# Dynamic convolution and squared-ReLU FFN on one core: band matmuls for the convolution, and a 64-row split of the first FFN matmul

## The chip, the cores and the metric

One core of a Trainium2 chip runs the whole program. The metric is device time in microseconds from start to end; lower is better. The engines named below work side by side, each through its own instructions in its own order, and wait for each other by semaphores: TensorE (PE, matmuls; PEld, its weight loads), VectorE (DVE), ScalarE (ACT), GpSimd (POOL) and SyncE (SP, which only issues DMA transfers here).

## What is computed

A causal convolution of 7 taps whose weights are different at each token and head, then an FFN with a squared ReLU. B = 8 sequences of S = 4096 tokens, D = 192 features in 8 heads of 24, FFN width 2048.

```
w = exp(weight_gen - max); w = w / sum(w)              # [B, S, 8 heads, 7 taps]
x_pad = 6 zero rows in front of x                      # [B, S + 6, 192]
y[b, s, h, g] = sum over k of w[b, s, h, k] * x_pad[b, s + k, 24 h + g]
h = maximum(y.reshape(32768, 192) @ w_in, 0)           # w_in  [192, 2048]
out = (h * h) @ w_out                                  # w_out [2048, 192]
```

## The kernel before

The 32768 tokens are cut into 64 blocks of 512 (8 per sequence); a block is four chunks of 128 tokens. One loop runs over blocks as a software pipeline: in one turn block `it` is loaded and its weights are normalised, block `it - 1` is convolved, block `it - 2` transposed, block `it - 3` goes through the first FFN matmul and block `it - 4` through the second.

The convolution has tokens on partitions. A transfer brings `x` seven times, shifted by one token each (`X6`, 128 x 7 x 192 per chunk, L112; at the start of a sequence seven transfers, L101). GpSimd normalises the weights (L129) and multiplies all seven copies by them (`pk`, L140, 1344 products per partition). VectorE adds the seven in three steps in place (L152 576, L155 384, L158 192 elements). TensorE transposes the sum, eight 128x128 pieces a block (L169), so that features lie on partitions, and ScalarE copies it out of PSUM (`yt`, L179). There are two `pk` buffers, and the transposes are their last readers, so a product waits for the transposes of two blocks before.

The FFN has features on partitions. The first matmul (mm1, L188) makes 16 chunks of 128 hidden units for 512 tokens; the 192 features are taken as 128 and as 64 that are padded with 64 zero rows of `w_in` to 128, so each chunk is two full matmuls, 32 a block. A pair of chunks is one `hps` tile of two PSUM banks (three buffers). ScalarE applies the ReLU to a pair (`t1`, L204, four buffers), VectorE squares it (`gT`, L209). The second matmul (mm2, L219) has a 128x128 piece of `gT` as weights and `w_out` as moving operand with 192 columns, 64 a block; ScalarE copies the result out (`o_sb`, L230) and SP stores it (L237).

The program is written stage by stage; a scheduling layer then orders the instructions of each engine and sets the waits. All transfers but the FFN weights go through SP's queue.

## Time and profile before

| | us |
|---|---|
| time, median of 2 runs (1389.41 and 1390.3) | 1389.86 |
| span of the profiled execution | 1387.2 |
| TensorE matmuls busy | 937.2 (68%) |
| VectorE busy | 1070.5 (77%) |
| ScalarE busy | 632.5 (46%) |
| GpSimd busy | 725.6 (52%) |
| moved by DMA | 211.26 MB, mean 152 GB/s |
| mean granted TensorE clock | 0.836 of full speed |

The span is that of one execution recorded by the profiler; the time is measured without it. Busy time counts an instruction from its start to its end, also where it is held up inside. A matmul's recorded length includes the time that its result takes to come out, so matmuls in a row overlap, and what a row of them costs is the step from one start to the next.

### The profile page before, as it was taken

How to read it: one execution, taken by the hardware profiler on the slowest of the kernel's cores; microseconds unless marked ns; L12 is line 12 of the kernel's file. 1: busy time of each engine (PE TensorE's matmuls, PEld its weight loads, DVE VectorE, ACT ScalarE, POOL GpSimd, SP SyncE). 2: the span in 40 equal slices, each digit the busy share in tenths (PEclk: the TensorE clock that was granted, in tenths of full speed). 3: DMA queues.
4: the chain of work that ended last, by engine and by line, in shares of the span. 5: the costliest groups of instructions: out<-in, count | busy, mean ns of one | idle time of the engine just before them, and what ended most of it. 6: DMA issues, size and time to landing. Idle time of an engine off the chain costs nothing.

```text
span 1387.2 us, 17548 instructions
## 1 busy us (share of the span) xinstructions
PE 937.2 (68%) x6656; PEld 627.6 (45%) x6656; DVE 1070.5 (77%) x1417; ACT 632.5 (46%) x769; POOL 725.6 (52%) x329
## 2 busy tenths in 40 slices
PE   0376666766766766767767668668667667677688
PEld 0144443544544544534535435435445445444456
DVE  2989778778787787787787787787887877877863
ACT  0244444544544544444444445445445445444455
POOL 3766545646546546456456455455465465464430
PEclk9888888878888888788788878888888888788899
DMA  8524456554443543444443443544434434434001
GB/s 240 218 101 153 144 194 242 192 176 143 159 179 120 173 177 128 166 143 144 181 161 129 166 167 139 183 149 140 177 137 158 176 119 177 173 107 179 15 24 41
DMA packets 114053, 211.26 MB, mean 152 GB/s; under 512 B 42264, under 2 KB 82032, under 8 KB 113968
## 3 DMA queue, kind: packets, MB, share of 16 engines
q1 hardware_dynamic: 111680, 208.57, 42.2%
q0 software_dynamic: 2288, 1.57, 0.8%
q8 instruction: 52, 0.85, 0.3%
q14 instruction: 33, 0.27, 0.1%
HBM read 186.52 MB, written 25.17 MB: 153 GB/s over the span
## 4 chain that ended last, share of the span: by engine, by line
DVE 52%; PE 25%; POOL 12%; ACT 6%; issue 3%; SPq 1%; DMA 1%; POOLq 0%; ACTq 0%; DVEq 0%
DVE pk L152 17%; DVE pk L155 16%; PE o L219 16%; DVE pk L158 13%; POOL pk L140 12%; PE hps L188 9%; DVE gT L209 5%; ACT t L204 4%; ACT o_sb L230 2%; SPq L112 1%; DMA wg<-in_weight_gen_dram 1%; SPq L101 1%; DVE ssum L121 0%; PE yps L169 0%; DVE rcp L124 0%
## 5 line engine op out<-in xcount | busy, mean ns | idle before, releaser
L140 POOL TENSOR_TENSOR pk<-X,nrm 128x1344 f16<-128x1344 f32 x256 | 672.1, 2655 | 511.5 <-ACT o_sb L230 469.0
L188 PE MATMUL hps<-yt,w_in 128*128 128x512 f16 x2048 | 526.3, 408 | 374.1 <-ACT t L204 373.0
L204 ACT ACTIVATE t<-hps 128x1024 f16<-128x1024 f32 x512 | 489.8, 1028 | 424.7 <-DVE gT L209 403.0
L188 PEld LDWEIGHTS <-w_in 128*128 128x128 f16 x2048 | 206.3, 101 | 620.7 <-issue 425.7
L152 DVE TENSOR_TENSOR pk<-pk 128x576 f16<-128x576 f16 x256 | 264.1, 1032 | 231.6 <-POOL pk L140 231.6
L219 PE MATMUL o<-w_out,gT 128*128 128x192 f16 x4096 | 421.3, 268 | 8.5 <-DVE gT L209 7.3
L219 PEld LDWEIGHTS <-gT 128*128 128x128 f16 x4096 | 395.3, 108 | 65.4 <-issue 45.4
L209 DVE TENSOR_TENSOR gT<-t 128x1024 f16<-128x1024 f16 x512 | 344.4, 711 | 28.3 <-ACT t L204 24.8
L155 DVE TENSOR_TENSOR pk<-pk 128x384 f16<-128x384 f16 x256 | 249.4, 974 | 6.3
L158 DVE TENSOR_TENSOR pk<-pk 128x192 f16<-128x192 f16 x256 | 207.5, 811 | 6.2
L230 ACT COPY o_sb<-o 128x384 f32<-128x384 f32 x128 | 61.2, 478 | 266.4 <-PE o L219 266.4
L129 POOL TENSOR_TENSOR nrm<-e,rcp 128x224 f32<-128x224 f32 x64 | 50.5, 789 | 91.8 <-DVE rcp L124 65.7
L169 PE MATMUL yps<-ident,pk 128*128 128x128 f16 x512 | 42.2, 222 | 63.9 <-DVE pk L158 63.9
L179 ACT COPY yt<-yps 128x1024 f16<-128x1024 f16 x64 | 64.8, 1012 | 31.6 <-PE yps L169 31.6
L169 PEld LDWEIGHTS <-pk 128*128 128x128 f16 x512 | 33.5, 98 | 69.8 <-POOL pk L140 59.0
L121 DVE TENSOR_REDUCE ssum<-e 128x32 f32<-128x224 f32 x64 | 24.2, 377 | 26.0 <-ACT e L117 26.0
L117 ACT ACTIVATE e<-wg 128x224 f32<-128x224 f32 x64 | 24.5, 383 | 28.3 <-DMA wg<-in_weight_gen_dram 28.3
L124 DVE RECIPROCAL rcp<-ssum 128x32 f32<-128x32 f32 x64 | 22.5, 352 | 5.3 <-DVE ssum L121 0.5
L98 DVE MEMSET X<- 6x1152 f32 x8 | 8.1, 1018 | 1.4 <-issue 1.2
L58 DVE MEMSET w_in<- 64x1024 uint32 x1 | 0.9, 912 | 1.0 <-PEq L298 1.0
L117 ACT ACT_TABLE_LOAD x1 | 1.3, 1283 | 0.7 <-PEq L298 0.7
L63 POOL DMA_DIRECT2D w_out<-in_moe_w_out_dram x1 | 1.2, 1208 | 0.0
(8 smaller groups left out, 2.2 us busy)
## 6 DMA issues: line engine op xcount, KB each, us to landing
X<-in_x_dram SPq DMA_DIRECT2D x248, 672.0 KB
out_dram<-o_sb SPq DMA_DIRECT2D x128, 192.0 KB
wg<-in_weight_gen_dram SPq DMA_DIRECT2D x64, 112.0 KB
X<-in_x_dram SPq DMA_DIRECT2D x8, 96.0 KB
w_out<-in_moe_w_out_dram POOLq DMA_DIRECT2D x1, 768.0 KB, 18.3
X<-in_x_dram SPq DMA_DIRECT2D x8, 95.2 KB
X<-in_x_dram SPq DMA_DIRECT2D x8, 94.5 KB
X<-in_x_dram SPq DMA_DIRECT2D x8, 93.8 KB
```

What stands on the lines that cost most here:

```text
L129: nc.gpsimd.tensor_tensor(out=nrm, in0=e_t[j], in1=rcp_t[j].unsqueeze(-1).broadcast_to((P, NCH, H, KK)), op=AluOp.mult,)
L140: nc.gpsimd.tensor_tensor(out=pk[:, c], in0=x6_t[j][:, c].rearrange("p k (h g) -> p k h g", h=H), in1=nrm_t[j][:, c] .rearrange("p h k -> ...
L152: nc.vector.tensor_tensor(out=v[:, 0:3, :], in0=v[:, 0:3, :], in1=v[:, 4:7, :], op=AluOp.add)
L155: nc.vector.tensor_tensor(out=v[:, 0:2, :], in0=v[:, 0:2, :], in1=v[:, 2:4, :], op=AluOp.add)
L158: nc.vector.tensor_tensor(out=v[:, 0], in0=v[:, 0], in1=v[:, 1], op=AluOp.add)
L169: nc.tensor.transpose(out=yps[:, ci, c * P : (c + 1) * P], in_=y16[:, dd0 : dd0 + P], identity=ident,)
L179: nc.scalar.copy(out=yt16, in_=yps)
L188: nc.tensor.matmul(out=hps[:, jj, :], lhsT=w_in16[ci][:, fc * P : (fc + 1) * P], rhs=yt16[:, ci, :], start=(ci == 0), stop=(ci == len(d_ch ...
L204: nc.scalar.activation(out=t1, in_=hps_t[(j, fp)], func=ActF.Relu)
L209: nc.vector.tensor_tensor(out=gT[:, 2 * fp : 2 * fp + 2, :], in0=t1, in1=t1, op=AluOp.mult)
L219: nc.tensor.matmul(out=o2[:, c % 2, :], lhsT=gT[:, fc, c * P : (c + 1) * P], rhs=w_out16[:, fc, :], start=(fc == 0), stop=(fc == NF - 1),)
L230: nc.scalar.copy(out=o_sb, in_=o2_t[(j, half)])
```

## The change

The convolution becomes a matmul. For a tile of tokens a band matrix `bd` is built per head: row = input token, column = output token, entry = the softmax weight of that pair where the two are 0 to 6 apart, else 0. With `x` of that tile as weights (tokens on partitions) the matmul gives y transposed at once, features on partitions. A block of 512 tokens is five tiles whose 128 input rows begin 98 tokens apart and which give 104, 104, 96, 96 and 112 outputs. A head has 24 features and TensorE's output places are 32 partitions wide, so each place takes two matmuls: all 32 rows with the later head's band, then the first 24, 16 or 8 rows again with the earlier head's, which overwrite. The last 64 features are made twice, on partitions 0 to 63 and 64 to 127. That is 5 x 16 = 80 matmuls a block, in four 32-column places.

The weights for the band are normalised for a whole sequence at once, written to `vbuf` in a skewed layout of 8 slots (slot = token modulo 8, so that a row's seven weights lie where its column has them), stored to a scratch tensor in DRAM (`vd`, SP) and read back per tile (`wr`, SP). VectorE multiplies them by a constant 0/1 `mask`, both operands repeated by access pattern, five products a block. `x` comes as 16-bit numbers through GpSimd's DMA queue, which converts. ScalarE's copy of y becomes a VectorE cast out of PSUM.

In mm1 the zero padding goes: the 64 rows of `w_in` stand twice in `w_b`, and the upper 64 features of the two chunks of a pair are two matmuls in the array's upper and lower 64 rows. The order is written anew as well: mm1 of a pair of chunks alternates with 8 matmuls of mm2 of the block before, and the convolution of the next block stands behind the sixth pair. PSUM: `h` two buffers of two banks (three before), `o` two (one before), `yp` one of two banks.

The lines that are only removed are those printed above. Of the new ones:

```diff
+    NT = 5
+    STEP = 98
+    BASE = -8
+    starts = [BASE + STEP * i for i in range(NT)]
+    bounds = [0, 104, 208, 304, 400, TB]
...
+    def load_weights():
+        nc.gpsimd.dma_start(out=w_a, in_=moe_w_in[0:P, :])
+        nc.gpsimd.dma_start(out=w_b[0:LO, :], in_=moe_w_in[P:D, :])
+        if ROW_TILED:
+            nc.gpsimd.dma_start(out=w_b[LO:P, :], in_=moe_w_in[P:D, :])
+        else:
+            nc.vector.memset(w_b[LO:P, :], 0.0)
+        nc.gpsimd.dma_start(out=w_o, in_=moe_w_out.rearrange("(c p) m -> p c m", p=P))
...
+    def st_softmax(b):
+        wg = wg_t[b]
+        v = vbuf[b % 2]
+        nc.scalar.activation(out=wg, in_=wg, func=ActF.Exp)
+        ssum = p_sm.tile([P, RH, H], f32, name="ssum")
+        nc.vector.tensor_reduce(out=ssum, in_=wg, axis=AxisX, op=AluOp.add)
+        rcp = p_sm.tile([P, RH, H], f32, name="rcp")
+        nc.vector.reciprocal(out=rcp, in_=ssum)
...
+            nc.vector.tensor_tensor(
+                out=vo,
+                in0=wg[:, i0 : i0 + n],
+                in1=rcp[:, i0 : i0 + n].unsqueeze(-1).broadcast_to((P, n, H, KK)),
+                op=AluOp.mult,
+            )
...
+    def st_load(j):
+        b, t0 = j // NBB, (j % NBB) * TB
+        xt = p_x.tile([P, NT, D], f16, name="xt")
+        wr = p_wr.tile([P, NT, H, SL], f16, name="wr")
+        x_t[j], wr_t[j] = xt, wr
+        wr2 = wr.rearrange("p t h c -> p t (h c)")
+        vd = vd_t[b]
...
+            else:
+                eng.dma_start(out=dst, in_=rows(src, t0 + BASE, width))
+
+    def st_band(j, i):
+        if i == 0:
+            bd_t[j] = p_bd.tile([P, H * TB], f16, name="bd")
+        lo, hi = bounds[i], bounds[i + 1]
+        n = hi - lo
+        m = mask[:, lo:hi]
+        if i == 0 and j % NBB == 0:
+            m = mask0
+        nc.vector.tensor_tensor(
+            out=bd_t[j][:, H * lo : H * hi].rearrange("p (h m c) -> p h m c", h=H, c=SL),
+            in0=wr_t[j][:, i].unsqueeze(2).broadcast_to((P, H, n // SL, SL)),
+            in1=m.rearrange("p (m c) -> p m c", c=SL)
+            .unsqueeze(1)
+            .broadcast_to((P, H, n // SL, SL)),
+            op=AluOp.mult,
+        )
+
+    G = D // H
+    quads = []
+    for q in range(D // 32):
+        ha, hb = (32 * q) // G, (32 * q + 31) // G
+        quads.append((q, ha, hb, hb * G - 32 * q))
+
+    def st_conv(j):
+        yp = ps_y.tile([P, 2, TB], f32, name="yp")
+        yp_t[j] = yp
+        places = [(q, 0, 32 * q) for q in range(4)]
+        places += [(q, 1, 32 * (q - 4)) for q in (4, 5)]
+        places += [(q, 1, 32 * (q - 2)) for q in (4, 5)]
+        for i in range(NT):
+            lo, hi = bounds[i], bounds[i + 1]
+            bd = bd_t[j][:, H * lo : H * hi].rearrange("p (h c) -> p h c", h=H)
+            for later in (True, False):
+                for q, ci, p0 in places:
+                    _, ha, hb, pre = quads[q]
+                    m = 32 if later else pre
+                    nc.tensor.matmul(
+                        out=yp[p0 : p0 + m, ci, lo:hi],
+                        lhsT=x_t[j][:, i, 32 * q : 32 * q + m],
+                        rhs=bd[:, hb if later else ha, :],
+                        start=True,
+                        stop=True,
+                        skip_group_check=True,
+                        tile_position=(0, p0),
...
+    def st_y_evac(j):
+        y = p_y.tile([P, 2, TB], f16, name="y")
+        y_t[j] = y
+        nc.vector.tensor_copy(out=y, in_=yp_t[j])
...
+            nc.tensor.matmul(
+                out=h[:, jj, :], lhsT=w_a[:, fc * P : (fc + 1) * P], rhs=y[:, 0, :],
+                start=True, stop=False,
+            )
...
+        if ROW_TILED:
+            for jj in range(2):
+                fc = 2 * fp + jj
+                r0 = LO * jj
+                nc.tensor.matmul(
+                    out=h[:, jj, :],
+                    lhsT=w_b[r0 : r0 + LO, fc * P : (fc + 1) * P],
+                    rhs=y[r0 : r0 + LO, 1, :],
+                    start=False, stop=True,
+                    tile_position=(r0, 0),
+                )
...
+    def st_mm2(j, part):
+        c, half = part // 2, part % 2
+        if part % 4 == 0:
+            o_t[(j, c // 2)] = ps_o.tile([P, 2, Dm], f32, name="o")
+        o = o_t[(j, c // 2)]
+        for fc in range(half * NF // 2, (half + 1) * NF // 2):
+                out=o[:, c % 2, :],
+                lhsT=g_t[j][:, fc, c * P : (c + 1) * P],
+                rhs=w_o[:, fc, :],
+                start=(fc == 0), stop=(fc == NF - 1),
+            )
...
+        for j in range(NBLK + 1):
+            nb = j // NBB + 1
+            if j < NBLK and nb < B:
+                if j % NBB == 0:
+                    st_wg_load(nb)
+                if j % NBB == 2:
+                    st_softmax(nb)
+            if j + 3 < NBLK:
+                st_load(j + 3)
+            for fp in range(NFP):
+                if j < NBLK:
+                    st_mm1(j, fp)
+                    st_relu(j, fp)
+                if j >= 1:
+                    st_mm2(j - 1, fp)
+                if j < NBLK:
+                    if j + 1 < NBLK:
+                        if fp < NT:
+                            st_band(j + 1, fp)
+                        if fp == NT:
+                            st_conv(j + 1)
+                            st_y_evac(j + 1)
+                    st_sq(j, fp)
```

TensorE, in the middle of a block. Before (`w_in_1` are the padded rows), where mm1 runs in one stretch:

```order
L219 MATMUL o_878<-w_out_68,gT 128x192
L188 LDWEIGHTS w_in_1_65
L188 MATMUL hps<-yt_690,w_in_1_65 128x512
L188 LDWEIGHTS w_in_0_63
L188 MATMUL hps<-yt_690,w_in_0_63 128x512
```

After, one pair of chunks and the beginning of its eight mm2 matmuls (`w_a` the 128 lower features, `w_b` the doubled 64 upper):

```order
L249 LDWEIGHTS w_a
L249 MATMUL h<-y,w_a 128x512
L262 LDWEIGHTS w_b
L262 MATMUL h<-y,w_b 128x512
L262 LDWEIGHTS w_b
L262 MATMUL h<-y,w_b 128x512
L289 LDWEIGHTS g
L289 MATMUL o<-w_o,g 128x192
```

Each pair now goes from full matmuls to two 64-row ones and back to full ones, where before all matmuls had the array whole.

TensorE where the convolution stands. Before, the eight transposes between two halves of mm2 (first one and what is ahead of it):

```order
L219 MATMUL o_818<-w_out_68,gT 128x192
L169 LDWEIGHTS pk
L169 MATMUL yps<-ident,pk 128x128
```

After, the convolution behind mm2's sixth part; 32 output rows first, 24, 16 and 8 later:

```order
L289 MATMUL o<-w_o,g 128x192
L228 LDWEIGHTS xt
L228 MATMUL yp<-bd,xt 32x104
L228 LDWEIGHTS xt
L228 MATMUL yp<-bd,xt 32x104
```

Eighty such pairs stand where eight transposes stood.

VectorE. Before, one piece of a block: adds on `pk` with squares between them:

```order
L152 TENSOR_TENSOR pk<-pk 128x576
L155 TENSOR_TENSOR pk<-pk 128x384
L158 TENSOR_TENSOR pk<-pk 128x192
L152 TENSOR_TENSOR pk<-pk 128x576
L209 TENSOR_TENSOR gT<-t_5637 128x1024
```

After, from the cast of the next block's y on (x2: two alike in a row; the first two squares are the last of a block, the third is the first of the next):

```order
L241 CAST y<-yp 128x1024
L200 TENSOR_TENSOR bd<-wr,mask 128x832 x2
L279 TENSOR_TENSOR g<-t_5480 128x1024
L200 TENSOR_TENSOR bd<-wr,mask 128x768 x2
L279 TENSOR_TENSOR g<-t_5496 128x1024
L200 TENSOR_TENSOR bd<-wr,mask 128x896
L279 TENSOR_TENSOR g<-t_5519 128x1024
```

The bands that belong to the block after next have moved up among the last squares of a block; the five other squares follow without anything between them.

## Rows read from the trace of the kernel before

**Rows 1.** Page, busy time by engine: us, share of span, instructions; span; DMA.
```profile
span 1387.2 us, 17548 instructions
PE 937.2 (68%) x6656; PEld 627.6 (45%) x6656; DVE 1070.5 (77%) x1417; ACT 632.5 (46%) x769; POOL 725.6 (52%) x329
...
DMA packets 114053, 211.26 MB, mean 152 GB/s; under 512 B 42264, under 2 KB 82032, under 8 KB 113968
```

**Rows 2.** Page, chain that ended last: shares of the span by line.
```profile
DVE pk L152 17%; DVE pk L155 16%; PE o L219 16%; DVE pk L158 13%; POOL pk L140 12%; PE hps L188 9%; DVE gT L209 5%; ACT t L204 4%; ACT o_sb L230 2%; SPq L112 1%; DMA wg<-in_weight_gen_dram 1%; SPq L101 1%; DVE ssum L121 0%; PE yps L169 0%; DVE rcp L124 0%
```

**Rows 3.** Timeline of one block: start, us, engine, line, work [idle before <-releaser].
```profile
697.80 2.50 DVE L158 TENSOR_TENSOR pk<-pk 128x192 f16<-128x192 f16 x1
...
701.36 0.26 DVE L158 TENSOR_TENSOR pk<-pk 128x192 f16<-128x192 f16 x1
...
703.74 4.00 ACT L204 ACTIVATE t<-hps 128x1024 f16<-128x1024 f32 x4 [6.70 <-DVE gT L209]
...
704.60 3.86 DVE L209 TENSOR_TENSOR gT<-t 128x1024 f16<-128x1024 f16 x6
704.81 1.87 PE L188 MATMUL hps<-yt,w_in 128*128 128x512 f16 x4 [6.41 <-ACT t L204]
...
706.47 4.08 PE L219 MATMUL o<-w_out,gT 128*128 128x192 f16 x32
...
710.39 0.61 PE L169 MATMUL yps<-ident,pk 128*128 128x128 f16 x8
...
711.09 10.46 POOL L140 TENSOR_TENSOR pk<-X,nrm 128x1344 f16<-128x1344 f32 x4 [9.98 <-ACT o_sb L230]
...
711.12 2.80 PE L219 MATMUL o<-w_out,gT 128*128 128x192 f16 x32
...
713.76 5.99 PE L188 MATMUL hps<-yt,w_in 128*128 128x512 f16 x27
```

**Rows 4.** Groups by line: work, count | busy us, mean ns | idle before, releaser.
```profile
L140 POOL TENSOR_TENSOR pk<-X,nrm 128x1344 f16<-128x1344 f32 x256 | 672.1, 2655 | 511.5 <-ACT o_sb L230 469.0 <-DMA X<-in_x_dram 20.9 <-issue 10.0
...
L152 DVE TENSOR_TENSOR pk<-pk 128x576 f16<-128x576 f16 x256 | 264.1, 1032 | 231.6 <-POOL pk L140 231.6
L155 DVE TENSOR_TENSOR pk<-pk 128x384 f16<-128x384 f16 x256 | 249.4, 974 | 6.3
L158 DVE TENSOR_TENSOR pk<-pk 128x192 f16<-128x192 f16 x256 | 207.5, 811 | 6.2
```

**Rows 5.** Windows: busy us by engine, granted TensorE clock, DMA share, GB/s.
```profile
0.00:50.00 50.00, 1.49 (x8) 0.65 (x9) 22.36 (x21) 2.43 (x4) 25.24 (x19) 1.00 0.84 261
428.00:554.00 126.00, 87.84 (x624) 59.05 (x624) 99.54 (x133) 59.19 (x72) 67.76 (x30) 0.83 0.44 156
726.20:727.80 1.60, 1.60 (x4) 0.50 (x4) 1.60 (x4) 1.60 (x2) 0.00 (x0) 0.50 0.98 373
734.70:740.60 5.90, 5.90 (x29) 2.64 (x28) 5.83 (x3) 4.25 (x5) 5.90 (x3) 1.00 0.10 33
```

**Rows 6.** Groups by line, continued: copies, normalisation and exp.
```profile
L179 ACT COPY yt<-yps 128x1024 f16<-128x1024 f16 x64 | 64.8, 1012 | 31.6 <-PE yps L169 31.6
L230 ACT COPY o_sb<-o 128x384 f32<-128x384 f32 x128 | 61.2, 478 | 266.4 <-PE o L219 266.4
L129 POOL TENSOR_TENSOR nrm<-e,rcp 128x224 f32<-128x224 f32 x64 | 50.5, 789 | 91.8 <-DVE rcp L124 65.7 <-ACT t L204 7.9 <-DVE pk L158 7.9
...
L117 ACT ACTIVATE e<-wg 128x224 f32<-128x224 f32 x64 | 24.5, 383 | 28.3 <-DMA wg<-in_weight_gen_dram 28.3
```

**Rows 7.** Softmax on VectorE by line: ns min/median/max, first and last start.
```profile
L121 DVE TENSOR_REDUCE ssum<-e x64: 366/379/387, 3.5 to 1255.8; 128x32 f32<-128x224 f32 x64
...
L124 DVE RECIPROCAL rcp<-ssum x64: 332/353/355, 3.9 to 1256.3; 128x32 f32<-128x32 f32 x64
```

**Rows 8.** TensorE by line, the same columns.
```profile
L188 PEld LDWEIGHTS <-w_in x2048: 95/98/152, 49.3 to 1373.8; 128*128 128x128 f16 x187
L188 PE MATMUL hps<-yt,w_in x2048: 376/379/635, 50.7 to 1374.0; 128*128 128x512 f16 x187
...
L219 PE MATMUL o<-w_out,gT x4096: 242/246/368, 69.4 to 1383.5; 128*128 128x192 f16 x196
...
L169 PE MATMUL yps<-ident,pk x512: 216/219/315, 36.6 to 1352.3; 128*128 128x128 f16 x171
```

**Rows 9.** Timeline at the two ends of the span.
```profile
0.75 0.44 SPq L89 DMA_DIRECT2D wg<-in_weight_gen_dram  x1
...
3.07 0.39 ACT L117 ACTIVATE e<-wg 128x224 f32<-128x224 f32 x1 [1.05 <-DMA wg<-in_weight_gen_dram]
...
50.70 0.59 PE L188 MATMUL hps<-yt,w_in 128*128 128x512 f16 x1 [1.10 <-ACT yt L179]
...
1383.78 0.48 ACT L230 COPY o_sb<-o 128x384 f32<-128x384 f32 x1 [2.89 <-PE o L219]
```

More of the change, by code (lines that the diff above doesn't have):

```diff
@@ L82 @@
-    t1_t, hps_t, o2_t, osb_t = ({} for _ in range(4))
-    def st_dma_in(j):
-        b = j // NBLK_PER_B
-        t0 = (j % NBLK_PER_B) * TB
-        wg = p_wg.tile([P, NCH, H, KK], f32, name="wg")
-        wg_t[j] = wg
+    ps_h = ctx.enter_context(tc.tile_pool(name="ps_h", bufs=2, space=bass.MemoryType.PSUM))
+    ps_o = ctx.enter_context(tc.tile_pool(name="ps_o", bufs=2, space=bass.MemoryType.PSUM))
+    w_a = const.tile([P, Dff], f16, name="w_a")
+    w_b = const.tile([P, Dff], f16, name="w_b")
@@ new lines, with band_mask @@
+    w_o = const.tile([P, NF, Dm], f16, name="w_o")
+    mask = const.tile([P, TB], f16, name="mask")
+    mask0 = const.tile([P, bounds[1]], f16, name="mask0")
+    vbuf = [const.tile([P, RH + KK - 1, H, SL], f16, name=f"v{i}") for i in range(2)]
+    def band_mask(t, shift):
+        n = t.shape[1]
+        nc.gpsimd.memset(t, 1.0)
+        nc.gpsimd.affine_select(
+            out=t, in_=t, pattern=[[1, n]], compare_op=AluOp.is_ge, fill=0.0,
+            base=shift, channel_multiplier=-1,
+        )
+        nc.gpsimd.affine_select(
+            out=t, in_=t, pattern=[[-1, n]], compare_op=AluOp.is_ge, fill=0.0,
+            base=KK - 1 - shift, channel_multiplier=1,
+        )
@@ new lines, in st_softmax @@
+    def st_softmax(b):
[6 more added lines that the diff above has]
+        nc.vector.reciprocal(out=rcp, in_=ssum)
+        pp = list(v.ap[0])
+        for i0 in range(0, RH, SL):
+            n = min(SL, RH - i0)
+            vo = bass.AP(
+                tensor=v.tensor, offset=v.offset + i0 * H * SL,
+                ap=[pp, [H * SL + 1, n], [SL, H], [H * SL, KK]],
+            )
+            nc.vector.tensor_tensor(
[3 more added lines that the diff above has]
+                op=AluOp.mult,
+            )
+        vd = p_dr.tile([S, H * SL], f16, name="vd")
+        vd_t[b] = vd
@@ new lines, in st_softmax, with rows @@
+            in_=v[:, KK - 1 : KK - 1 + R].rearrange("p r h c -> p (r h c)"),
+        )
+    x_t, wr_t, bd_t, yp_t, y_t, g_t, h_t, t1_t, o_t = ({} for _ in range(9))
+    def rows(ap2d, t0, width):
+        return bass.AP(
+            tensor=ap2d.tensor, offset=ap2d.offset + t0 * width,
+            ap=[[width, P], [STEP * width, NT], [1, width]],
+        )
+    def st_load(j):
[5 more added lines that the diff above has]
+        vd = vd_t[b]
+        for dst, src, width, eng in (
+            (wr2, vd, H * SL, nc.sync),
+            (xt, x[b], D, nc.gpsimd),
+        ):
+            if t0 == 0:
+                eng.dma_start(out=dst[:, 0], in_=src[0:P, :])
+                first = rows(src, BASE + STEP, width)
+                first = bass.AP(
+                    tensor=first.tensor, offset=first.offset,
+                    ap=[first.ap[0], [STEP * width, NT - 1], first.ap[2]],
+                )
+                eng.dma_start(out=dst[:, 1:NT], in_=first)
+            else:
+                eng.dma_start(out=dst, in_=rows(src, t0 + BASE, width))
@@ L211, in st_sq @@
         )
-    def st_mm2(j, c):
-        gT = g_tile(j)
-        if c % 2 == 0:
-            o2_t[(j, c // 2)] = ps_o.tile([P, 2, Dm], f32, name="o2")
-        o2 = o2_t[(j, c // 2)]
-        for fc in range(NF):
-            nc.tensor.matmul(
-                out=o2[:, c % 2, :],
-                lhsT=gT[:, fc, c * P : (c + 1) * P],
-                rhs=w_out16[:, fc, :],
-                start=(fc == 0),
-                stop=(fc == NF - 1),
-            )
-    def st_o_evac(j, half):
-        o_sb = p_os.tile([P, 2, Dm], f32, name="o_sb")
-        osb_t[(j, half)] = o_sb
-        nc.scalar.copy(out=o_sb, in_=o2_t[(j, half)])
@@ new lines @@
+    with nc.allow_low_precision("fp16 matmul pipeline"):
+        st_wg_load(0)
+        for v in vbuf:
+            nc.vector.memset(v, 0.0)
+        band_mask(mask0, 0)
+        for i in range(NT):
+            band_mask(mask[:, bounds[i] : bounds[i + 1]], bounds[i] - starts[i])
+        st_softmax(0)
+        st_load(0)
+        load_weights()
+        st_load(1)
+        st_load(2)
+        for i in range(NT):
+            st_band(0, i)
+        st_conv(0)
+        st_y_evac(0)
+        for j in range(NBLK + 1):
[21 more added lines that the diff above has]
+                    st_sq(j, fp)
```

231 lines of the change are left out of this document (56 added, 175 removed).

## The prediction, made before the changed kernel ran

> **What bounds the kernel now.** I read the page's busy table first. VectorE is the busiest engine with 1070.5 us of 1387.2, TensorE 937.2, GpSimd 725.6, ScalarE 632.5 [rows 1]: no engine is full, so something makes them wait for each other. The chain that ended last says where: the three adds on `pk` (L152, L155, L158) hold about 47% of it and GpSimd's product (L140) 12%, against 25% for all of TensorE's two matmul lines [rows 2].
>
> The timeline of one block (20.7 us from the product at 700 to the next) shows the loop [rows 3]. GpSimd starts four products at 711.09 and needs 10.46 us. While they run, an add of 192 elements on VectorE takes 2.50 us (697.80); the same add with GpSimd idle takes 0.26 us (701.36). So VectorE and GpSimd do not overlap: beside a product VectorE gets through one small instruction per product. When the products end, VectorE still has most of the adds and the squares of the FFN to do; ScalarE's ReLU (703.74) waits 6.70 us for a square, TensorE (704.81) waits 6.41 us for the ReLU, TensorE then runs mm2, 4.08 us, and the transposes (710.39), and only these free `pk` for the next product. 10.46 us of product, then about 10.3 us of adds, ReLU, mm1, mm2 and transposes in a row: that is the period. The grouped rows say it over the whole run: the product costs 672.1 us and stood idle 511.5 us before that; the adds have means of 1032, 974 and 811 ns for 576, 384 and 192 elements, hardly falling with their size [rows 4].
>
> The windows show TensorE's clock: a mean of 0.83 over six blocks; 0.50 (1.2 GHz) just after the 6.4 us of idling, 1.00 (2.4 GHz) in the dense stretch behind it [rows 5].
>
> **What the change removes.** The product and its normalisation (672.1 + 50.5 us of GpSimd), the three adds (264.1 + 249.4 + 207.5 us of VectorE), the transposes and their copy (64.8 us of ScalarE) [rows 1, 4, 6]. All of GpSimd's arithmetic goes, so the loop above is gone, and the seven-fold copies of `x` with it. What is left is a pipeline in which each engine works in its own order; the period becomes the work of the busiest engine in a block.
>
> **ScalarE per block.** Eight ReLUs, unchanged: four in 4.00 us [rows 3], so 8.0; two copies of 0.478 [rows 6] make 1.0; `exp` of 2128 elements once in 8 blocks: 224 elements take 0.383 us [rows 6], at most 9.5 times that, 3.6/8 = 0.5. Sum 9.5 us.
>
> **VectorE per block.** Eight squares, six in 3.86 us [rows 3], 0.643 each: 5.1. Five band products of 768 to 896 16-bit elements are not in the trace. If they go as the squares do, 832/1024 x 0.643 = 0.52 each, 2.6; if they go one element per step as the reduction does (224 in 0.379 us, 1.7 ns per element [rows 7]), 1.4 each, 7.0. They are two-input products of 16-bit numbers as the squares are: I take 0.6 each, 3.0. The cast of 1024 values out of PSUM: between a square (0.64) and that reduction (1.7); 1.2. Softmax of 2128 weights per 8 blocks: reduction 3.6, reciprocal of 304 at 32 in 0.353 [rows 7] 3.4, products of 448 at that rate 5 x 0.8: 11.0/8 = 1.4 at most. Sum 10.7 us, ends 9.7 and 15.2.
>
> **TensorE per block.** Full 128x512 matmuls: 27 in 5.99 us [rows 3]; less the last one's length of 0.379 [rows 8], 26 steps of 0.216. The second FFN matmul: 32 in 2.80 us, less 0.246, 31 steps of 0.0824; 64 of them 5.27 us, unchanged in number. mm1 changes from four full steps per pair of chunks (0.864) to two full ones and a pair of 64-row ones. If the pair runs at once it costs one step, 0.216; if in turn, 0.432. I take one step, as their outputs, weights and input rows are disjoint. Eight pairs: 8 x 0.648 = 5.18 us (in turn 6.91).
>
> The convolution is new: 80 matmuls of 96 to 112 columns with 8 to 32 outputs, each with a weight load. The nearest row is the eight transposes (128 columns, a weight load each) in 0.61 us: seven steps of 0.056 behind one of 0.219 [rows 3, 8]. By that 80 x 0.056 = 4.5 us; if four 32-column places work at once, a quarter, 1.1. The loads take as long as anything here, 0.098 us each [rows 8], so I take a good part in turn: 3.0 us.
>
> The Trainium skill, TensorE: Matmul & The Clock Gate, Part 3, gives 2.38x for three column tiles at 512 columns; an estimate by it is 4.5/2.38 = 1.9 us, 1.1 us a block less than I take. No run here shows it yet.
>
> Then the **switch of shape**. Twice per pair (to 64-row tiles and back) and twice at the convolution, 18 times a block, the array changes how it is cut. Nothing in before does this. Bounds from rows: nothing, if the stream goes on; or the stream stops until the last matmul has come out and the next weights are in. A matmul lasts 0.379 where a step is 0.216, so 0.163 comes after its stream, and a load is 0.098 [rows 8]: 0.261 together. Between them I take 0.163, the row nearest to emptying an array: 18 x 0.163 = 2.9 us; ends 0 and 4.7.
>
> The Trainium skill, TensorEngine Tiling (Array Packing), Tiling Modes, states that changing the tiling mode, not just the tile, drains TensorE, and that different tiles can load and multiply in parallel. By the first half the pairing, which gives back 0.216 x 8 = 1.7 us, pays for 16 drains, 2.6 us at my price; by a free switch the block would be 2.9 us shorter.
>
> Sum: 5.27 + 5.18 + 3.0 + 2.9 = **16.4 us**; ends 11.6 (all free) and 21.4 (6.91 + 5.27 + 4.5 + 4.7). TensorE is therefore the bound, ahead of VectorE's 10.7 and ScalarE's 9.5. Both of these stay hidden in it: `h` has two buffers and `t1` four, and the order puts the bands of block j+2 among block j's last squares. The cast of `y` queues squares behind it until the convolution is over, but mm2 wants the last square only two mm1 pairs into the next block, about 5 us later, against 4 us of VectorE work. With a gapless TensorE the clock stays at 1.00.
>
> **Transfers.** Per block: output 393 KB, `x` 492 KB (read once more for the overlap of tiles, not seven times), weights 285 KB through a scratch in DRAM: 1.2 MB in 16 us, 72 GB/s, against 152 GB/s on average now and 373 in one stretch [rows 1, 5]. Loads stand three blocks ahead, on SP and on GpSimd's queue. I cost them at nothing; if a load came late the cover is 48 us.
>
> **Ends.** Before: first mm1 matmul at 50.70 us [rows 9], as the 7-fold `x` had to come first. After: 1.09 MB of weights (about 7 us, at the 261 GB/s of the first 50 us [rows 5]), `exp` 2 to 3.6, softmax, where the order does two batches at once (12 to 20), scratch out and in (two trips; `wg` came in some 2 us [rows 9]), bands and convolution (6): about 40 us, ends 33 and 50. The first block has no mm2 (-4). Behind the last block: 64 x 0.0824 = 5.3, the copy 0.48, and 2.9 us from the last copy's end to the span's end [rows 1, 9]: 9 us.
>
> Total: 40 + 64 x 16.4 - 4 + 9 = 1095 us of span. The span of before is 1387.2 and the runs' median 1389.86, 2.7 more; so **1097 us**.
>
> **Rivals.**
> - *Everything on TensorE is free* (no drain, pairs and column places at once): 11.6 us, and then VectorE and ScalarE, 10.7 and 9.5, are as near; with their waits 12 to 13.5 a block, 815 to 910 us. For it: TensorE's steps in before show no gap between unlike matmuls (32 of mm2 follow mm1 without one). Against: those all have the same shape.
> - *Pairs in turn and the full price of a switch*: 19 to 20.4 us, 1265 to 1350 us. For it: weight loads of 0.098 us are in the stream and cannot lie under a matmul of another shape if the array must be empty.
> - *Slower than before*: the switch costs more than its bound. No change means (1387.2 - 45)/64 = 20.97 us a block; 20.97 - 13.45 = 7.5 us for 18 switches, **0.42 us each**, 1.6 times emptying plus load. From there on the kernel is slower; at 0.5 us, 22.5 us a block, about 1485 us. Against it: nothing in the rows lasts that long but a cold matmul (0.635 at most [rows 8]).
> - *No change*: VectorE waits for GpSimd as before. Against: GpSimd issues transfers only.
>
> **How the numbers follow.** My case, 14.3 to 18.5 us a block: 0.63, 960 to 1232 us. All free: 0.18. In turn: 0.12. Slower: 0.05. No change: 0.02. The predicted time is the likeliest's. Leaving out the lower half of the free case and the upper part of the others, the range is **890 to 1250 us**. Faster by over 2% (2% is about what a measurement of this kernel can tell from no change): all but the last two, 0.92; within 2%: 0.03; slower: 0.05.
>
> **What would show it.** GpSimd under 60 us busy and no square over 0.8 us: the loop is gone. A stretch of 8 mm2 matmuls starting within 0.05 us behind the 64-row pair: the switch is free; 0.16 to 0.26 us later: my price. The pair starting together: concurrent; 0.216 apart: in turn. Convolution 3 us a block, TensorE's clock 1.00, TensorE the chain's main engine. I am wrong if VectorE's bands take over 1.4 us, if TensorE waits for a transfer, or if the 64-row or 32-column matmuls let the granted clock fall to 0.50.

## The result and the profile after

The changed kernel takes **958.24 us** (median of two, 957.37 and 959.11) against 1389.86: a ratio of 0.689, interval 0.687 to 0.691. The forecast was 1097, the range 890 to 1250. The profiled execution has a span of 955.7 us and a mean granted clock of 0.975.

From the page of the changed kernel, first the span, the busy time of each engine (us, share of the span, instructions) and the chain that ended last, by engine and by line; these answer to [rows 1, 2]:

```profile
span 955.7 us, 25454 instructions
PE 863.3 (90%) x11264; PEld 504.9 (53%) x11264; DVE 686.6 (72%) x955; ACT 587.3 (61%) x649; POOL 64.9 (7%) x98
...
PE 79%; DVE 16%; DMA 3%; issue 1%; ACT 1%; SPq 0%; ACTq 0%; DVEq 0%
PE o L289 37%; PE h L249 21%; PE h L262 15%; DVE v L147 8%; PE yp L228 6%; DVE g L279 3%; DMA wg<-in_weight_gen_dram 2%; DVE bd L200 2%; DVE rcp L139 1%; DVE ssum L137 1%; DVE y L241 1%; DMA wr<-vd 1%; ACT t L273 0%; DMA vd<-v 0%; ACT wg L135 0%
```

Before, VectorE's adds and GpSimd's product held 58% of the chain [rows 2]. Now TensorE holds 79% and is busy for 90% of the span. GpSimd's 64.9 us are nearly all issues of transfers, most of them those of `x`:

```profile
L190 POOL DMA_DIRECT2D xt<-in_x_dram x56 | 47.8, 856 | 710.5 <-PE yp L228 671.9 <-PE h L262 38.6
```

The groups of VectorE and ScalarE (work, count | busy us, mean ns | idle before, releaser), to be held against [rows 4, 6, 7]:

```profile
L273 ACT ACTIVATE t<-h 128x1024 f16<-128x1024 f32 x512 | 523.3, 1023 | 303.1 <-PE h L262 283.1
L279 DVE TENSOR_TENSOR g<-t 128x1024 f16<-128x1024 f16 x512 | 353.3, 693 | 245.2 <-ACT t L273 242.6
...
L200 DVE TENSOR_TENSOR bd<-wr,mask 128x832 f16<-128x832 f16 (+2 forms) x320 | 173.2, 576 | 6.8 <-DMA wr<-vd 6.8
...
L241 DVE CAST y<-yp 128x1024 f16<-128x1024 f32 x64 | 79.2, 1237 | 2.5
L147 DVE TENSOR_TENSOR v<-wg,rcp 128x448 f16<-128x448 f32 (+1 forms) x40 | 79.9, 2142 | 0.1
...
L137 DVE TENSOR_REDUCE ssum<-wg 128x304 f32<-128x2128 f32 x8 | 18.8, 2346 | 4.7 <-ACT wg L135 4.7
```

ScalarE waits for TensorE, VectorE for ScalarE: the waits run down the pipeline from one busy engine. One block on TensorE (timeline; from the first convolution to the next one is a block):

```profile
501.79 0.59 PE L249 MATMUL h<-y,w_a 128*128 128x512 f16 x2
502.31 0.39 PE L262 MATMUL h<-y,w_b 64*128 64x512 f16 x2
502.63 0.83 PE L289 MATMUL o<-w_o,g 128*128 128x192 f16 x8
503.31 0.59 PE L249 MATMUL h<-y,w_a 128*128 128x512 f16 x2
...
504.15 0.83 PE L289 MATMUL o<-w_o,g 128*128 128x192 f16 x8
504.92 1.09 PE L228 MATMUL yp<-bd,xt 128*32 128x104 f16 x80
505.94 0.61 PE L249 MATMUL h<-y,w_a 128*128 128x512 f16 x2
...
518.20 1.09 PE L228 MATMUL yp<-bd,xt 128*32 128x104 f16 x80
```

A block is 518.20 - 504.92 = 13.28 us, against (1387.2 - 45)/64 = 20.97 before. A pair of chunks takes 503.31 - 501.79 = 1.52 us. The two 64-row matmuls last 0.39 us together, as long as one full matmul alone (0.379 [rows 8]): they run at once. The convolution takes 505.94 - 504.92 = 1.02 us, and 504.92 - 504.15 less eight mm2 steps of 0.0824 leaves 0.11 in front of it: 8 x 1.52 + 1.13 = 13.29.

The windows (busy us of PE, PEld, DVE, ACT, POOL with instructions; granted clock; DMA share; GB/s) show where this pace does not yet hold:

```profile
0.00:47.60 47.60, 2.52 (x80) 1.91 (x81) 35.24 (x26) 7.50 (x5) 11.39 (x32) 1.00 0.80 182
47.60:205.00 157.40, 114.09 (x1358) 61.62 (x1357) 150.87 (x159) 79.78 (x84) 7.27 (x9) 0.85 0.36 84
205.00:946.00 741.00, 740.90 (x9762) 436.03 (x9761) 499.77 (x771) 498.03 (x559) 46.20 (x57) 1.00 0.30 54
```

From 205 us on TensorE is busy 740.90 of 741.00 us at a clock of 1.00. From 47.6 to 205 us it stands idle for 43.3 us, its clock is 0.85, and VectorE is the full engine (150.87 of 157.40).

### The profile page after: what moved, and what is told of

It is laid out like the page before. It is cut to its first block, busy times and chain, and to the rows that moved or that the text cites. A ratio compares the mean times of both kernels' runs of the same rounds, so it can differ in the third digit from the quotient of the medians.

```text
span 955.7 us, 25454 instructions
## 1 busy us (share of the span) xinstructions
PE 863.3 (90%) x11264; PEld 504.9 (53%) x11264; DVE 686.6 (72%) x955; ACT 587.3 (61%) x649; POOL 64.9 (7%) x98
## 4 chain that ended last, share of the span: by engine, by line
PE 79%; DVE 16%; DMA 3%; issue 1%; ACT 1%; SPq 0%; ACTq 0%; DVEq 0%
PE o L289 37%; PE h L249 21%; PE h L262 15%; DVE v L147 8%; PE yp L228 6%; DVE g L279 3%; DMA wg<-in_weight_gen_dram 2%; DVE bd L200 2%; DVE rcp L139 1%; DVE ssum L137 1%; DVE y L241 1%; DMA wr<-vd 1%; ACT t L273 0%; DMA vd<-v 0%; ACT wg L135 0%
## 5 line engine op out<-in xcount | busy, mean ns | idle before, releaser
L273 ACT ACTIVATE t<-h 128x1024 f16<-128x1024 f32 x512 | 523.3, 1023 | 303.1 <-PE h L262 283.1
L279 DVE TENSOR_TENSOR g<-t 128x1024 f16<-128x1024 f16 x512 | 353.3, 693 | 245.2 <-ACT t L273 242.6
L289 PE MATMUL o<-w_o,g 128*128 128x192 f16 x4096 | 430.0, 249 | 0.3 <-DVE g L279 0.2
L289 PEld LDWEIGHTS <-g 128*128 128x128 f16 x4096 | 314.9, 98 | 117.0 <-issue 115.8
L249 PE MATMUL h<-y,w_a 128*128 128x512 f16 x1024 | 309.8, 385 | 45.1 <-DVE y L241 39.0
L262 PE MATMUL h<-y,w_b 64*128 64x512 f16 x1024 | 201.3, 390 | 0.0
L200 DVE TENSOR_TENSOR bd<-wr,mask 128x832 f16<-128x832 f16 (+2 forms) x320 | 173.2, 576 | 6.8 <-DMA wr<-vd 6.8
L249 PEld LDWEIGHTS <-w_a 128*128 128x128 f16 x1024 | 88.2, 98 | 54.4 <-DVE y L241 39.6
L241 DVE CAST y<-yp 128x1024 f16<-128x1024 f32 x64 | 79.2, 1237 | 2.5
L147 DVE TENSOR_TENSOR v<-wg,rcp 128x448 f16<-128x448 f32 (+1 forms) x40 | 79.9, 2142 | 0.1
L137 DVE TENSOR_REDUCE ssum<-wg 128x304 f32<-128x2128 f32 x8 | 18.8, 2346 | 4.7 <-ACT wg L135 4.7
L139 DVE RECIPROCAL rcp<-ssum 128x304 f32<-128x304 f32 x8 | 16.1, 2022 | 0.0
L308 DVE MEMSET v<- 128x1408 uint32 x2 | 2.5, 1232 | 1.4 <-PEq L358 1.2
```

Source lines behind the costliest of these rows:

```text
L137: nc.vector.tensor_reduce(out=ssum, in_=wg, axis=AxisX, op=AluOp.add)
L147: nc.vector.tensor_tensor(out=vo, in0=wg[:, i0 : i0 + n], in1=rcp[:, i0 : i0 + n].unsqueeze(-1).broadcast_to((P, n, H, KK)), op=AluOp.mult,)
L200: nc.vector.tensor_tensor(out=bd_t[j][:, H * lo : H * hi].rearrange("p (h m c) -> p h m c", h=H, c=SL), in0=wr_t[j][:, i].unsqueeze(2).bro ...
L241: nc.vector.tensor_copy(out=y, in_=yp_t[j])
L249: nc.tensor.matmul(out=h[:, jj, :], lhsT=w_a[:, fc * P : (fc + 1) * P], rhs=y[:, 0, :], start=True, stop=False,)
L262: nc.tensor.matmul(out=h[:, jj, :], lhsT=w_b[r0 : r0 + LO, fc * P : (fc + 1) * P], rhs=y[r0 : r0 + LO, 1, :], start=False, stop=True, tile ...
```

## Experiments

Four questions: what the gain is made of, what the 64-row split does, why the convolution is so short, and what the first 205 us cost. The kernel before took 1389.5 to 1389.6 us beside each of them. A time with its extremes behind it is the median of four runs, the others are of one run each. Unless something else is said, a code cut shows the edit to the changed kernel, with `...` for lines left out.

### What the gain is made of

**The kernel before, its products on VectorE** (one word of the kernel before, L140):

```diff
-        nc.gpsimd.tensor_tensor(
+        nc.vector.tensor_tensor(
             out=pk[:, c],
```

> The kernel before with its four products a block moved from GpSimd to VectorE; nothing else is changed. Theory, VectorE stood still beside each product: without it the adds take 0.45, 0.36 and 0.26 us, 4.3 us a block, the squares 5.1, softmax 0.7, the products about 1.5 each, 6: 16.1 us of VectorE a block, 17 to 19 with the loop's waits, 1130 to 1270 us although VectorE has more to do. Rival, GpSimd's share is real help and VectorE is simply full: 1070.5 us of VectorE and 64 x 6 more, 1450 to 1770.

Measured: 1063.06 us. Its page, busy times and groups:

```profile
PE 870.7 (82%) x6656; PEld 572.9 (54%) x6656; DVE 956.8 (90%) x1673; ACT 613.4 (58%) x769; POOL 180.2 (17%) x73
...
L140 DVE TENSOR_TENSOR pk<-X,nrm 128x1344 f16<-128x1344 f32 x256 | 400.2, 1601 | 22.0 <-DMA X<-in_x_dram 22.0
...
L129 POOL TENSOR_TENSOR nrm<-e,rcp 128x224 f32<-128x224 f32 x64 | 177.1, 2767 | 823.6 <-DVE rcp L124 700.7
...
L152 DVE TENSOR_TENSOR pk<-pk 128x576 f16<-128x576 f16 x256 | 111.5, 455 | 0.0
...
L155 DVE TENSOR_TENSOR pk<-pk 128x384 f16<-128x384 f16 x256 | 83.2, 344 | 0.0
...
L158 DVE TENSOR_TENSOR pk<-pk 128x192 f16<-128x192 f16 x256 | 57.6, 244 | 0.0
```

VectorE took over 400.2 us of products, and its own busy time fell from 1070.5 to 956.8 us, because the adds went from 264.1, 249.4 and 207.5 us [rows 4] to 111.5, 83.2 and 57.6, with means that now fall with the size. So most of the length of the adds was time held up beside GpSimd's products, not work. By itself this one word is worth 1389.6 - 1063.1 = 326.5 us, three quarters as much as the whole change's 431.6; the two are not parts of one sum, since the change does away with the products and the adds as well. The normalisation that stayed on GpSimd shows the other side: 0.789 us each before [rows 6], 2.767 beside a VectorE that now has products of its own. The kernel is now bound by VectorE (90% busy); the convolution as matmul takes that work away.

**GpSimd products put back into the changed kernel.** Six products of 1024 elements a block whose output nobody reads:

```diff
+    scr = const.tile([P, 2, TB], f16, name="scr")
+
+    def st_pool(j):
+        nc.gpsimd.tensor_tensor(out=scr, in0=y_t[j], in1=y_t[j], op=AluOp.mult)
...
                 if j < NBLK:
+                    if fp < 6:
+                        st_pool(j)
                     st_mm1(j, fp)
```

> The changed kernel with six products of 1024 elements a block added on GpSimd; they read y and write a tile that nobody reads, so only GpSimd's work comes back, with no wait of another engine for its result. Theory, a two-input instruction on VectorE cannot run beside a GpSimd product: the products take about 2 us each (2.66 for 1344 before), 12 us a block in which VectorE gets through only one instruction per product; a block needs 13 two-input instructions and the cast, so 12 + 7 x 0.6 + 1.2 = 17.5 us a block instead of 13.3, about 1220 us, and the squares' mean goes from 0.69 us to over 1. Rival, the engines do not touch each other and only the old loop's waits were removed: 958.

Measured: 1533.57 us, slower than the kernel before. Groups by line, then rows of its timeline near the start and in the middle:

```profile
L246 POOL TENSOR_TENSOR scr<-y 128x1024 f16<-128x1024 f16 x384 | 827.5, 2155 | 133.1 <-DVE y L241 107.9
...
L294 PE MATMUL o<-w_o,g 128*128 128x192 f16 x4096 | 512.8, 271 | 400.1 <-DVE g L284 400.1
L284 DVE TENSOR_TENSOR g<-t 128x1024 f16<-128x1024 f16 x512 | 578.6, 1152 | 192.4 <-ACT t L278 192.2
L200 DVE TENSOR_TENSOR bd<-wr,mask 128x832 f16<-128x832 f16 (+2 forms) x320 | 576.7, 1836 | 6.7 <-DMA wr<-vd 6.7
```

```profile
58.01 6.82 POOL L246 TENSOR_TENSOR scr<-y 128x1024 f16<-128x1024 f16 x3
...
63.00 1.21 DVE L241 CAST y<-yp 128x1024 f16<-128x1024 f32 x1
```

```profile
810.79 0.69 DVE L284 TENSOR_TENSOR g<-t 128x1024 f16<-128x1024 f16 x1 [0.83 <-ACT t L278]
...
812.98 13.22 POOL L246 TENSOR_TENSOR scr<-y 128x1024 f16<-128x1024 f16 x6 [0.28 <-DVE y L241]
815.44 2.38 DVE L284 TENSOR_TENSOR g<-t 128x1024 f16<-128x1024 f16 x1
```

A square lasts 0.69 us with GpSimd idle and 2.38 beside a product; the bands go from 0.576 to 1.836; TensorE's mm2, which had waited 0.2 us for squares, waits 400.1. The mechanism is that of before, its price larger than expected (1220 us). Squares and bands together take (578.6 + 576.7)/64 = 18.1 us a block where 16.2 had been counted; the softmax, (79.9 + 18.8 + 16.1)/64 = 1.8 us a block, had been left out; and VectorE stands idle for 192.4/64 = 3.0 us a block, because a late square holds up TensorE and the next ReLU comes late.

The cast, whose one input is in PSUM, rarely meets a product in this run: each block's products wait for its cast, and 62 of the 64 casts run with no product beside them. The two that do lie inside a product keep their length; one is shown, 1.21 us from 63.00 on, within the last of three products that end at 64.83. The Trainium skill, SBUF — State Buffer, Who interferes with whom, states that a VectorE instruction with two SBUF inputs contends with a GpSimd instruction that reads SBUF, and that one with at most one such input, outside VectorE's two-port modes, does not: the traces agree on both, the squares and bands by the first, those two casts by the second.

### What the 64-row split does

**All matmuls of mm1 with 128 rows again** (the upper 64 rows of `w_b` zero):

```diff
-ROW_TILED = True
+ROW_TILED = False
```

> The 64-row pair is undone: each chunk is two full matmuls again, the upper 64 features padded with 64 zero rows of weights; everything else as in the changed kernel. Theory: in the changed kernel a pair of chunks takes 0.52 us until the 64-row pair starts (two full steps of 0.216 and a switch of 0.09) and 0.32 from there to the second FFN matmul (one step and a switch of 0.10), 0.84 in all; four full steps are 0.864. So 512 x 0.024 = 12 us slower, 970 us. Rival A, the switch costs nothing that counts and the pair saves a full step: 512 x 0.216 = 110 us slower, 1068. Rival B, the prediction's price, two switches of 0.163 against one step of 0.216: 56 us faster, 902.

Measured: 960.15 us (959.52 to 961.29), ratio to before 0.691, interval 0.690 to 0.692; the changed kernel's 0.687 to 0.691 overlaps it. That is 1.9 us more, where 12 were expected. One pair of chunks in its timeline:

```profile
501.43 0.38 PE L249 MATMUL h<-y,w_a 128*128 128x512 f16 x1
501.65 0.38 PE L254 MATMUL h<-y,w_b 128*128 128x512 f16 x1
501.86 0.38 PE L249 MATMUL h<-y,w_a 128*128 128x512 f16 x1
502.08 0.38 PE L254 MATMUL h<-y,w_b 128*128 128x512 f16 x1
502.29 0.82 PE L289 MATMUL o<-w_o,g 128*128 128x192 f16 x8
502.95 0.38 PE L249 MATMUL h<-y,w_a 128*128 128x512 f16 x1
```

The pair takes 502.95 - 501.43 = 1.52 us here too: four steps of 0.216 instead of three, but no gaps. In the changed kernel `w_b` starts 0.52 us behind `w_a`, two steps and 0.09; mm2 starts 0.32 us behind `w_b`, one step and 0.10; and its eight matmuls take 503.31 - 502.63 = 0.68 us where they take 0.66 here, the 0.02 that the expectation did not count. The step that the split saves, 0.216, is what its two switches of shape cost, 0.21. The split as made gives nothing that can be measured.

**Both 64-row matmuls in the same rows.** Shape and number stay, only the concurrency goes:

```diff
-                r0 = LO * jj
+                r0 = 0
```

> Both 64-row matmuls of a pair take the array's lower 64 rows, with the copies of features and weights that lie there; the switches stay, only the two places become one. Theory, the two run at the same time only because they stand in different rows: one step of 0.216 more for each of 512 pairs, 110 us, about 1068. Rival, they run in turn already and the pair's short time has another cause: 958, no change.

Measured: 1057.83 us. In its timeline:

```profile
501.86 0.59 PE L249 MATMUL h<-y,w_a 128*128 128x512 f16 x2
502.38 0.60 PE L262 MATMUL h<-y,w_b 64*128 64x512 f16 x2
502.92 0.83 PE L289 MATMUL o<-w_o,g 128*128 128x192 f16 x8
```

The two now last 0.60 us together, and mm2 follows 0.54 behind the first instead of 0.32. 99.6 us more over 512 pairs is 0.195 each, about one step (0.22 in the rows): the pair is concurrent, because its rows are different.

**One return trip for two pairs of chunks.** mm1 of two pairs as full, 64-row, 64-row, full, then 16 mm2 matmuls:

```diff
+        low(f0, True)
+        up(f0, False)
+        up(f0 + 1, True)
+        low(f0 + 1, False)
...
-            for fp in range(NFP):
+            for f0 in range(0, NFP, 2):
```

> Two pairs of chunks are taken together: full, 64-row, 64-row, full, then 16 matmuls of the second FFN matmul; same work, half the switches for the 64-row tiles. Theory, a return trip costs 0.19 us: 4 fewer a block, 64 x 4 x 0.19 = 49 us faster, 909. Rival A, the prediction's price of 0.163 a switch: 84 us faster, 874. Rival B, the two h buffers now come free too late and TensorE waits for ScalarE's two ReLUs (2 x 1.0 us): 958 or more, with waits of TensorE for ReLU in the rows.

Measured: 908.83 us (908.21 to 910.03), ratio 0.654, interval 0.653 to 0.655. 49.4 us over 64 blocks of four saved return trips is 0.193 us a return trip. That is a mean over all blocks, also the first eight or so, whose pace TensorE does not set. Two pairs in the middle of the run:

```profile
501.30 0.59 PE L251 MATMUL h<-y,w_a 128*128 128x512 f16 x2
...
504.12 0.59 PE L251 MATMUL h<-y,w_a 128*128 128x512 f16 x2
```

They take 504.12 - 501.30 = 2.82 us instead of 2 x 1.52, and a block, from one convolution to the next, 12.43 instead of 13.28: 0.85 for four, **0.21 us a return trip**, 0.11 a switch, the same as the gaps in the timeline. With half the switches the split does pay: 908.8 against 960.2 with full rows in pairs. Full rows taken two pairs at a time were not run; that grouping has nothing to save there is argued, from rows without a gap.

### Why the convolution is so short

**Place by place.** The ten matmuls of a 32-column place in a row, instead of going round the places:

```diff
-        for i in range(NT):
...
-            for later in (True, False):
-                for q, ci, p0 in places:
+        for q, ci, p0 in places:
...
+            for i in range(NT):
...
+                for later in (True, False):
```

> The same 80 matmuls of the convolution, ordered so that ten in a row write the same 32-column place, where before the place changed with each. Theory, four places run at once, which is why 80 matmuls take 1.02 us: ten in one place must go in turn, 80 x 0.046 (104 columns at 2.4 GHz and the step's rest, from the transposes' 0.056 for 128) = 3.7 us a block, 64 x 2.7 = 172 us slower, 1130. Rival, the rate is that of issuing a load and a matmul (0.013 us a pair) whatever the place: 958.

Measured: 1049.60 us. The convolution and the matmul that follows it:

```profile
516.93 2.62 PE L228 MATMUL yp<-bd,xt 128*32 128x104 f16 x80
519.48 0.60 PE L249 MATMUL h<-y,w_a 128*128 128x512 f16 x2
```

2.55 us instead of 1.02: the order matters, but 0.032 us a matmul is less than the 0.046 that a place was expected to take, so it left open whether matmuls in one place overlap.

**Each place's ten done three times over** (240 matmuls; the repeats write the same numbers; the cut is against the run above):

```diff
         for q, ci, p0 in places:
             _, ha, hb, pre = quads[q]
-            for i in range(NT):
+            for i in 3 * list(range(NT)):
```

> The convolution ordered by place, each place's ten matmuls done three times over (same results), 240 instead of 80. By place, 80 took 2.55 us, 0.032 each, where 104 columns at 2.4 GHz need 0.043. Theory, a place runs one column a cycle and what was saved lies at the seven changes of place, where the next place starts before the one ahead is through: 240 x 0.043 less the same 0.9 us, 9.4 us, 64 x 8.4 = 538 us more, about 1495. Rival, matmuls in one place overlap by themselves and 0.032 is their step: 240 x 0.032 = 7.7, 64 x 6.6 = 424 more, about 1385.

Measured: 1503.19 us, the theory's 1495 and not the rival's 1385. The convolution:

```profile
805.76 9.85 PE L228 MATMUL yp<-bd,xt 128*32 128x104 f16 x240
815.54 0.61 PE L249 MATMUL h<-y,w_a 128*128 128x512 f16 x2
```

453.6 us more than the kernel above over 64 x 160 matmuls is 0.0443 us each, and 815.54 - 805.76 = 9.78 us against 2.55 is 0.0452; at the pace of the full matmuls, 0.216 us for 512 columns, the 102.4 columns of a mean tile would take 0.043. So inside a place matmuls go one after another, and the 3.54 - 2.55 = 1.0 us that the kernel above is below 80 x 0.0443 is left to the seven changes of place. The single records of that kernel's trace agree: the first steps in a place are 0.042 to 0.057 us, and then the next place's first matmuls start among the last four of the one before. In the changed kernel's, four matmuls start within 0.01 us of each other and the next four 0.03 to 0.05 later. Going round four places, 80 x 0.0443 = 3.54 us becomes 1.02: 3.5 of at most 4.

### What the first 205 us cost

All eight softmaxes lie before 205 us: `wg` of a later sequence is loaded as soon as its buffer is free, and its softmax is placed ahead of the bands that TensorE needs. In the changed kernel's timeline VectorE spends 19.03 us in products of two sequences before the first mm1 can start, and the last product of the last sequence starts at 198.01 us:

```profile
16.56 19.03 DVE L147 TENSOR_TENSOR v<-wg,rcp 128x448 f16<-128x448 f32 x10
...
47.61 1.01 PE L249 MATMUL h<-y,w_a 128*128 128x512 f16 x2 [2.04 <-DVE y L241]
...
198.01 1.68 DVE L147 TENSOR_TENSOR v<-wg,rcp 128x336 f16<-128x336 f32 x1
```

**Weights in time.** The load of a sequence's `wg` waits for the first block of the sequence before:

```diff
+        if after is not None:
+            nc.vector.tensor_copy(out=wg[:, 0, 0, 0:1], in_=y_t[after][:, 0, 0:1])
...
-                    st_wg_load(nb)
+                    st_wg_load(nb, j)
```

> The changed kernel with each sequence's weights loaded only when the sequence before it begins (a one-element copy of that block's y into the tile stands ahead of the load); the softmax work is the same, but spread over the run instead of done by 200 us. Theory, between 47 and 205 us VectorE is busy 151 of 158 us with the softmax of all sequences and TensorE loses about 49 us there (8.2 blocks in place of 11.9), and before the first matmul two softmaxes are done where one is needed (13 us); 15 us of softmax per 8 blocks fit into the 4 us a block that VectorE has left. 62 us less at most: 896 to 915. Rival, the work in a burst stops TensorE each time, 7 times 7 us: only the start is won, about 945.

Measured: 936.91 us (936.61 to 937.82), ratio 0.674, interval 0.673 to 0.675. A gain of 21.3 us, not the 43 to 62 of the theory. The first mm1 and one window in which a softmax lies:

```profile
32.79 1.01 PE L251 MATMUL h<-y,w_a 128*128 128x512 f16 x2 [2.04 <-DVE y L243]
```

```profile
240.00:260.00 20.00, 20.00 (x303) 12.04 (x303) 14.87 (x25) 12.91 (x16) 1.71 (x2) 1.00 0.39 70
260.00:280.00 20.00, 16.19 (x196) 8.83 (x193) 16.97 (x18) 12.10 (x13) 0.86 (x1) 1.00 0.34 89
```

14.8 us are won at the start. The rest of the loss moved: each softmax, wherever it stands, is some 14 us of VectorE in one piece with squares queued behind, and TensorE loses 3.8 us in the second window and 1.2 in the next. Eight blocks with a softmax among them take 5.7 to 7.0 us longer here than eight of 13.28. The rival was mostly right.

**Heads innermost in the softmax product**, to test whether its write pattern makes it long:

```diff
-                ap=[pp, [H * SL + 1, n], [SL, H], [H * SL, KK]],
+                ap=[pp, [H * SL + 1, n], [H * SL, KK], [SL, H]],
...
-                in0=wg[:, i0 : i0 + n],
-                in1=rcp[:, i0 : i0 + n].unsqueeze(-1).broadcast_to((P, n, H, KK)),
+                in0=wg[:, i0 : i0 + n].rearrange("p n h k -> p n k h"),
+                in1=rcp[:, i0 : i0 + n].unsqueeze(2).broadcast_to((P, n, KK, H)),
```

> The softmax product of 448 elements walks its output with heads innermost (16 bytes apart) instead of taps (128 bytes apart); same elements, same results. Theory, the write step is what makes it 2.1 us, 4.8 ns an element, where the reduction takes 1.1: it falls under 1.2 us; 40 products x 1 us, nearly all of it in the stretch in which VectorE is the bound, about 40 us less, 918. Rival, the 32-bit inputs and the broadcast set it: 958.

Measured: 957.91 us; a product takes 2139 ns in the mean instead of 2142. Going from 128 to 16 bytes between writes gains nothing. That is not yet proof against the writes: 16 bytes still leave every element apart from the next, and the inputs are now read in another order too, which could take back a gain. Why a product of 448 elements takes 2.2 us, about 5 ns an element (the mean of 2142 mixes in eight of 336), stays open.

**Softmax in pieces, and two pairs at a time.** The grouped mm1, the late load, and the products of the softmax held to four blocks; of the edit, the last part:

```diff
+                if j % NBB == 1:
+                    st_sums(nb)
+                if 1 <= j % NBB <= 4:
+                    for i0 in {1: (0,), 2: (SL,), 3: (2 * SL,), 4: (3 * SL, 4 * SL)}[j % NBB]:
+                        st_piece(nb, i0, j)
+                if j % NBB == 4:
+                    st_store(nb)
```

> Two pairs of chunks at a time as in the run that halved the switches, the weights of a sequence loaded in time, and the five products of its softmax held to four successive blocks (a one-element copy of that block's y stands ahead of each). Theory, what cost 7 us a sequence with the weights loaded in time was the burst of 15 us of softmax on VectorE, not its sum: 909 less 15 at the start and 49 behind it, 845 us, up to 865 if a single product still delays a square. Rival, TensorE's shorter block leaves VectorE no room and it waits for squares wherever a product stands: 880 to 895.

Measured: **854.56 us** (850.4 to 857.52), ratio 0.616, interval 0.614 to 0.617; 103.7 us less than the changed kernel. The two windows that answer to those above, from the fastest of the four runs (span 848.7 us):

```profile
60.00:200.00 140.00, 138.38 (x1950) 87.01 (x1949) 119.98 (x179) 98.19 (x112) 10.27 (x13) 1.00 0.37 74
200.00:830.00 630.00, 622.05 (x8788) 390.86 (x8788) 504.31 (x755) 443.09 (x505) 41.46 (x51) 1.00 0.35 70
```

TensorE is busy 138.38 of 140 us in the stretch where it had lost most, and its clock there is 1.00. The early loss is gone. What the pieces won by themselves was not run apart from the grouping; but eight blocks with a softmax among them now take 1.7 to 2.3 us longer than eight of 12.43, where the burst cost 5.7 to 7.0.

## Why the prediction was right, and where its numbers were off

**The bound and the loop: right.** The forecast read a stand-off of VectorE and GpSimd out of one pair of rows, 2.50 and 0.26 us for the same add [rows 3]. Both experiments on it show it as the cause, and TensorE became the bound as said. Of its signs these came out: the longest part of the chain is TensorE's, the clock is 1.00 (from 205 us on), the 64-row pair starts together. Two missed their limits: GpSimd is at 64.9 us and not under 60, nearly all of it issues; and 10 of 512 squares last over 0.8 us (median 0.691, longest 0.922). The two that carried my prices, of the switch and of the convolution, did not come out. One reading was a slip on which nothing hangs: the products of two blocks start at 689.74 and 711.09 us in the trace of before, 21.35 apart and not 20.7.

**The block: two terms of the sum were too large.** By its own working 16.4 us; measured 13.28.

| per block, us | predicted | measured |
|---|---|---|
| eight pairs: mm1, mm2 and 16 switches | 5.18 + 5.27 + 16 x 0.163 = 13.06 | 8 x 1.52 = 12.16 |
| convolution and two switches | 3.0 + 0.33 = 3.33 | 1.13 |

- *The convolution* failed by 2.2 us a block. The step was "I take a good part in turn", because a weight load of 0.098 us is as long as anything there. It rested on the transposes, whose steps have one place the size of the array. The low end, a quarter of 4.5 us, was the right one. The Trainium skill, TensorE: Matmul & The Clock Gate, Part 3, with 2.38x for three places, gave an estimate of 1.9 us, nearer than my 3.0; here four places give 3.5x over one.
- *The switch* was priced at 0.163 us, "the row nearest to emptying an array", and costs 0.09 to 0.11: between nothing and that. The Trainium skill, TensorEngine Tiling (Array Packing), Tiling Modes, states that a change of mode drains TensorE; the trace agrees that there is a stop, and 0.163, the time by which a full matmul outlasts its step, is more than the whole of it. The weighing in the forecast, 1.7 us given back by the split for 2.6 us of switches, comes out as 1.7 for 8 x 0.21 = 1.7.

Together 64 x 3.12 = 200 us too much.

**The ends: two terms were too small.** With the measured block the forecast's own sum would be 47.6 + 64 x 13.28 - 4 + 9 = 902.5 us of span, with the measured start in place of 40; the span is 955.7. The start is 8 us late because the two batches of softmax took VectorE from 7.82 to 35.59 us, 27.8 where 12 to 20 had been put; the load in front of them was put too high, since 1.09 MB at 261 GB/s are 4.2 us and not 7. The missing 53 us lie between 47.6 and 205 us, 43.3 of them idle TensorE; the rest I put down to its clock of 0.85 there. The step that failed is the softmax as "11.0/8 = 1.4 at most", a mean spread over eight blocks. One softmax is 2.35 + 2.02 (the reciprocal) + 79.9/8 = 14.4 us, since its products take 2.1 us and not 0.8, and it comes in one piece; and the order let eight of them run in the first 205 us, where VectorE was the bound. The forecast had seen two batches before the first mm1, and not that the others follow at once. The sum of all: 1095 - 200 + 8 + 53 = 956.

So the errors had opposite signs and partly cancelled, which is luck: with the block's error alone the forecast would have been 200 us too high, with that of the ends alone 61 too low. The time fell just below the likeliest case's own range (960 to 1232), in the gap to the free case, and 139 us under the forecast.

**What was costed right.** VectorE: 686.6/64 = 10.7 us a block (10.7), its parts less well (the squares 5.5 for 5.1, the softmax 1.8 for 1.4); bands 0.576 each (0.6); cast 1.237 (1.2); ScalarE 587.3/64 = 9.2 (9.5). The cast and the squares queued behind it do not stop TensorE, which is busy 740.90 of 741 us. Transfers hide: DMA is 3% of the chain, two thirds of it the loads of `wg`.

**The rivals.** Pairs in turn: no, and the run that forces it is 99.6 us slower. Everything free: 11.6 us a block is not reached, since the 16 switches of the pairs cost 1.7. Slower than before: it needed 0.42 us a switch, about four times what one costs. No change: shown false by the page.

## What to carry to other kernels

When the same small instruction is many times longer beside another engine's work than alone, price the removal of that neighbour first: moving the products to the *same* engine that was already the busiest gave by itself three quarters as much as the whole change. A split of the array has to save more than its two switches (0.21 us here), so group what has the same shape before splitting, and go round the places rather than finishing one. Work that comes once in eight blocks is a burst and not a mean: ask what stands behind it in its engine's queue, and when the order lets it begin.
